# An ordered filter kept in memory, half of a transposition sent through memory, and scaled matrices made beside their use

## The chip, the cores and the metric

The kernel runs on one core of one Trainium2 chip. The metric is the device time of one execution in microseconds (us), as the median of several executions.

## The reference, cut to what matters

```python
def A(x, w_r, w_i):                       # spectral layer
    X = rfft2(x)                          # over S = 2048 and D = 1024
    X = X * (w_r + 1j * w_i)              # one filter, 2048 x 513
    return irfft2(X, s=(S, D)).astype(bf16)

def B(x, w1, b1, w2):                     # dense layer, F = 3584
    h = x @ w1 + b1
    return (h * tanh(log1p(exp(-abs(h))) + where(h > 0, h, 0))) @ w2

x = x + A(layernorm(x), w_r, w_i)
x = x + B(layernorm(x), w1, b1, w2)
x = x + A(layernorm(x), w_r, w_i)         # the same filter again
x = x + B(layernorm(x), w1, b1, w2)
```

All tensors are bf16. The second spectral layer uses the same filter as the first; this is what the first part of the change builds on.

## The kernel before

The transforms are matrix products with small tables. A spectral layer has a first step `s1`, then a software pipeline of 12 steps over 8 filter groups, then a last transform `i4` with the residual. In the first layer the layernorm's 1/std is folded into `s1` as 128 scaled copies of one 128x128 matrix. Helpers compute the waits of each operation from what it reads and writes. The helper for a DMA puts the DMA's waits into the program of the engine that issues it, so whatever comes later in that program stands behind them. In the trace GpSimd was held so for 10.2 us in two waits, 5.8 us the longest, by stores to xn_scratch.

```python
def first_scales(self):                   # first layer: statistics, then ALL scaled matrices
    ...
    for j in range(16):
        for q in range(8):                # every third on ScalarE, the others on VectorE
            ...  self.MN[n] = self.M0 * rc[n]

def load_w(g):                            # raw filter, ring of 4
    ...
    for c, src in enumerate((self.w_r, self.w_i)):
        rows = src.rearrange("(k s) d -> k s d", s=16)[:, a:b + 1:b - a, 1:513]
        self.dma(pool, wr.ap[:, c, :, :], rows, f"wr{g % 4}", parts=[wr.res])

def filter_bins(g):                       # raw filter -> ordered filter WT
    ...                                   # 12 matmuls of 128x64 turn a part around
    for i in range(2):
        ...
        self.op(pool, lambda e, d3=d3, lo=lo: e.tensor_copy(d3[:, :, :, 0:64], lo[:, :, 0:3, :]), ...)
        self.op(pool, lambda e, dd=dd, lo=lo: e.tensor_copy(dd, lo[:, :, 3:8:4, :]), ...)
        self.op(act, lambda e, d3=d3, src=src: e.activation(d3[:, :, :, 64:128], src, ACT.Copy), ...)

# s3: 4 matmuls (table FT), ScalarE evicts x, VectorE multiplies by the filter
    ta = x * wt[:, 0:1, :]; tb = x * wt[:, 1:2, :]      # two-input, 128x1024
    yk[:, 0] = ta[:, 0] - tb[:, 1]; yk[:, 1] = tb[:, 0] + ta[:, 1]
# i1 (table BT) and i2: inverse; VectorE evicts half 0 of U, ScalarE half 1

def u_turn(g, half):                      # row r of U becomes partition r*8+g of UT
    for i in range(8):
        r = 8 * half + i
        prog = sp
        if g == 7 and i % 2:
            prog = act
        elif g < 7 and i % 4 == 3:
            prog = pool
        self.dma(prog, self.UT.ap[r * 8 + g:r * 8 + g + 1, :, :], u.ap[:, r, :], ...)   # 32 KB

for step in range(8 + 4):
    g2, g3, g4, g5 = step, step - 1, step - 3, step - 4
    for h in range(2):
        s2(g2, h); filter_bins(g2) if h == 0; s3(g3, h); i1(g4, h); i2(g5, h); u_turn(g5, h)
    load_tabs(g3 + 2); load_w(g2 + 4); load_btabs(g4 + 2)     # all in GpSimd's queue
while self.w1_next < 28 * li + 4:
    self.load_w1()                        # first weights of the dense layer, SyncE
```

(Bounds checks are left out. Each u_turn row is a copy from SBUF to SBUF.)

## Time and profile before

| | before |
|---|---|
| median of 3, lowest, highest | 1152.24, 1148.83, 1152.91 us |
| span of the profiled execution | 1148.9 us |
| first step of layer 1 ends (first `s2` matmul) | 60.5 us |
| loop of layer 1, to its last inverse group / to `i4` | 91.6 / 17.8 us |
| from there to the first step of layer 2 (mainly dense 1) | 435.0 us |
| loop of layer 2 / to `i4` | 89.5 / 20.9 us |

The stage times are differences of start times in the timeline of TensorE. The list of waits has the engine, its line, what it waited for, then the sum, the count and the longest in us:

```profile
PE PS L700 <- DMA ARENA<-c_bt: 15.0, 4, 4.5
PE PS L813 <- DMA ARENA<-ARENA: 37.5, 2, 20.3
```

TensorE waits for tables (c_bt) in the loops, never for more than 4.5 us, and for up to 20.3 us at the end of a spectral layer, for the last rows of the turn.

### The profile page before, as it was taken

What the parts mean: (1) busy time and instruction counts of PE and PEld (TensorE: products, weight loads), DVE (VectorE), ACT (ScalarE), POOL (GpSimd) and SP (SyncE); (2) the same over time, 40 slices, a digit from 0 to 9 for tenths busy, and PEclk for the clock granted to TensorE, in tenths of its full rate; (3) what the DMA queues carried; (4) which work ended last, traced back from release to release, by engine and by line L of the source; (5) the groups of instructions that cost most, each with busy time, mean ns of one, the idle gap of its engine ahead of it and who ended that gap; (6) DMA issues with size and microseconds to landing.
All of it is one profiled execution on the core that took longest, in us unless ns stands there. A gap on an engine that the chain in (4) does not pass through costs nothing.

```text
span 1148.9 us, 14586 instructions
## 1 busy us (share of the span) xinstructions
PE 981.6 (85%) x6091; PEld 522.5 (45%) x6185; DVE 383.5 (33%) x813; ACT 332.9 (29%) x466; POOL 139.6 (12%) x204
## 2 busy tenths in 40 slices
PE   0388636999999999999958884489999999999998
PEld 0366524444444444444427663344444444444443
DVE  4877518250244400024326971546001110000111
ACT  6566515333100043400006662243320003442000
POOL 2165400000000000001343651000000000000000
PEclk9999968999999999999988997699999999999999
DMA  9634892344200022101971369713440002210000
GB/s 299 144 84 83 87 99 64 111 145 148 83 19 19 28 74 76 35 10 31 117 157 45 92 91 70 120 59 125 149 145 19 28 19 64 74 55 1 28 19 28
DMA packets 133105, 90.26 MB, mean 79 GB/s; under 512 B 56560, under 2 KB 114160, under 8 KB 133040
## 3 DMA queue, kind: packets, MB, share of 16 engines
q1 hardware_dynamic: 121600, 68.16, 25.3%
q0 software_dynamic: 8560, 20.52, 9.6%
q10 hardware_dynamic: 2880, 0.66, 1.3%
q8 instruction: 49, 0.80, 0.3%
q14 instruction: 16, 0.13, 0.0%
HBM read 72.46 MB, written 8.13 MB: 70 GB/s over the span
## 4 chain that ended last, share of the span: by engine, by line
PE 72%; DVE 13%; DMA 5%; SPq 4%; ACT 3%; issue 2%; ACTq 0%; POOL 0%; DVEq 0%
PE PS L886 33%; PE PS L868 32%; SPq L242 4%; DMA ARENA<-ARENA 2%; DMA XS<-in_A_x_dram 2%; DVE ARENA L682 2%; PE PS L605 1%; DVE ARENA L539 1%; PE PS L633 1%; DVE BN L427 1%; DVE XS L819 1%; PE PS L850 1%; DVE ARENA L689 1%; DVE ARENA L560 1%; DVE ARENA L684 1%
## 5 line engine op out<-in xcount | busy, mean ns | idle before, releaser
L868 PE MATMUL PS<-ARENA 128*128 128x512 bf16 x1752 | 385.3, 379 | 5.5 <-DVE ARENA L855 2.0
L886 PE MATMUL PS<-ARENA 128*128 128x512 bf16 x1754 | 387.4, 379 | 2.0
L872 ACT ACTIVATE ARENA<-PS,B 128x512 bf16<-128x512 f32 x224 | 153.6, 688 | 437.4 <-PE PS L868 437.4
L868 PEld LDWEIGHTS PS<-ARENA 128*128 128x128 bf16 x1792 | 174.4, 98 | 212.5 <-DVE ARENA L855 1.9
L886 PEld LDWEIGHTS PS<-ARENA 128*128 128x128 bf16 x1792 | 174.6, 98 | 207.7
L891 DVE TENSOR_TENSOR XS<-PS,XS 128x512 bf16<-128x512 f32 x64 | 44.3, 692 | 565.5 <-PE PS L886 565.5
L427 DVE BATCH_NORM_STATS2 BN<-XS 128x6 f32<-128x512 bf16 x104 | 67.1, 674 | 11.4 <-DMA XS<-in_A_x_dram 10.1
L242 POOL DMA_DIRECT2D ARENA<-xn_scratch x15 | 15.9, 1068 | 417.1 <-PE PS L886 388.3
L813 PE MATMUL PS<-MT,ARENA 128*128 128x32 bf16 (+1 forms) x768 | 24.6, 188 | 45.7 <-DMA ARENA<-ARENA 37.5
L819 DVE TENSOR_TENSOR XS<-PS,XS 128x512 bf16<-128x512 f32 (+1 forms) x40 | 29.1, 789 | 87.8 <-PE PS L813 87.8
L558 ACT ACTIVATE ARENA<-PS 128x1024 bf16<-128x1024 f32 x16 | 15.9, 1021 | 124.2 <-PE PS L552 124.0
L700 PE MATMUL PS<-ARENA 128*128 128x256 bf16 x256 | 37.5, 295 | 15.0 <-DMA ARENA<-c_bt 15.0
L813 PEld LDWEIGHTS PS<-MT,ARENA 128*128 128x128 bf16 x768 | 23.0, 101 | 49.1 <-issue 41.6
L408 ACT ACTIVATE ARENA<-XS 128x1024 bf16<-128x1024 bf16 x24 | 25.4, 1056 | 56.2 <-DVE XS L819 40.8
L707 ACT ACTIVATE ARENA<-PS 128x1024 bf16<-128x1024 f32 x32 | 32.6, 1020 | 24.1 <-PE PS L700 24.1
L700 PEld LDWEIGHTS PS<-ARENA 128*128 128x128 bf16 x256 | 26.6, 105 | 25.4 <-issue 15.8
L242 POOL DMA_DIRECT2D ARENA<-ARENA x56 | 30.2, 543 | 65.1 <-DVE ARENA L747 52.4
L682 DVE TENSOR_TENSOR ARENA<-ARENA 128x1024 bf16<-128x1024 bf16 x32 | 30.2, 943 | 23.1 <-ACT ARENA L678 23.0
L678 ACT ACTIVATE ARENA<-PS 128x1024 bf16<-128x1024 f32 x32 | 32.7, 1023 | 17.7 <-PE PS L674 17.7
L721 PE MATMUL PS<-ARENA,BD 128*128 128x256 bf16 x192 | 28.8, 293 | 9.5 <-DVE ARENA L747 9.2
L633 PE MATMUL PS<-FD,ARENA 128*128 128x256 bf16 (+1 forms) x312 | 34.0, 258 | 2.8 <-DVE ARENA L560 2.4
L613 POOL COPY ARENA<-ARENA 128x384 bf16<-128x384 bf16 x32 | 29.4, 920 | 10.4 <-DVE ARENA L684 10.4
(65 smaller groups left out, 621.6 us busy)
## 6 DMA issues: line engine op xcount, KB each, us to landing
ARENA<-in_B_w_dram SPq DMA_DIRECT2D x56, 512.0 KB, 3.9
ARENA<-in_B_w_dram SPq DMA_DIRECT2D x56, 256.0 KB, 4.5
ARENA<-ARENA SPq DMA_DIRECT2D x188, 32.0 KB, 6.6
XS<-in_A_x_dram SPq DMA_DIRECT2D x4, 1024.0 KB, 15.6
ARENA<-in_A_w_r_dram POOLq DMA_DIRECT2D x16, 256.0 KB, 4.1
ARENA<-in_A_w_i_dram POOLq DMA_DIRECT2D x16, 256.0 KB, 4.9
ARENA<-in_A_x_dram SPq DMA_DIRECT2D x32, 128.0 KB, 3.1
out_dram<-XS SPq DMA_DIRECT2D x16, 256.0 KB, 2.0
```

The costliest lines, as they stand in the source:

```text
L242: return eng.dma_start(out_ap, in_ap).then_inc(ds.sem, 16)
L427: self.op(self.dve, lambda e: e.bn_stats(self.BN[:, j, 6 * h:6 * h + 6], self.XS[:, j, 512 * h:512 * h + 512]), reads=[self.r_xs[j]], part ...
L633: fns.append(lambda e: e.matmul(dst, at(r), FD[:, t:t + dst.shape[-1] * 2], start=start, stop=stop))
L678: self.op(act, lambda e: e.activation(x.ap.rearrange("p a b -> p (a b)"), ps, ACT.Copy, scale=SIG), reads=banks, writes=[x.res])
L682: self.op(dve, lambda e: e.tensor_tensor(ta.ap, x.ap, wt.ap[:, 0:1, :].to_broadcast([P, 2, 512]), ALU.mult), reads=[x.res, wt.res], writes ...
L700: fns.append(lambda e, c=c, part=part: e.matmul(ps[:, c * 256:(c + 1) * 256], yk.ap[:, part, c * P:(c + 1) * P], t[:, (128, 0)[part]:(384, ...
L813: fns.append(lambda e, l=l: e.matmul(ps[:, w * l:w * l + w], self.UT.ap[:, u0 + l, :], self.MT[:, 8 * lo:8 * lo + w], start=True, stop=True))
L819: self.op(self.dve, lambda e: e.tensor_tensor(xs, src, xs, ALU.add), reads=rb, parts=self.r_xs[lo:lo + nb])
L868: fns.append(lambda e, db=db, bank=bank, fl=fl: e.matmul(PS[:, bank, :], wb.ap[:, db, fl * P:(fl + 1) * P], x.ap[:, db, :], start=(db == 0 ...
L872: self.op(act, lambda e, bank=bank, ft=ft: e.activation(at.ap[:, ft, :], PS[:, bank, :], ACT.Mish, bias=self.B1[:, ft:ft + 1]), reads=[sel ...
L886: fns.append(lambda e, i=i, ft=ft: e.matmul(PS[:, bank, :], at.ap[:, ft, t * P:(t + 1) * P], W2[ft].ap[:, h * 512:(h + 1) * 512], start=(i ...
L891: self.op(dve, lambda e: e.tensor_tensor(xs, PS[:, bank, :], xs, ALU.add), reads=[self.r_bank[bank]], writes=[self.r_xs[j]])
```

## The change

It has three parts. **Front:** the first filter loads wait until x is there, the statistics go ten to VectorE and six to ScalarE, and the scaled matrices are made four groups ahead inside `s1` instead of all before it; the ring of ordered filters grows from 4 to 8 buffers and that of raw ones shrinks from 4 to 2. **Kept filter:** during the first dense layer the filter is ordered once more, stored to memory, and loaded in order in layer 2, whose loop has no `filter_bins`. **Turn through memory:** for groups 0 to 6 the second half of the rows (eight of 16) is stored by SyncE to a scratch tensor, and one load by GpSimd brings it back onto eight partitions, in place of eight row copies. For odd groups ScalarE evicts half 0 as well.

```diff
 # front, s1
+        for j in range(4 if not li else 0):
+            self.scaled(j)
         for j in range(16):
             ...                                  # 8 matmuls, one eviction
+            if not li and j + 4 < 16:
+                self.scaled(j + 4)
 # rings
-        WT = ring("WT", 4, 2 * K, [2, 512])
+        WT = ring("WT", 8, 2 * K, [2, 512])
-        WR = ring("WR", 4, 4 * K, [2, 2, 512])
+        if li == 0:
+            WR = ring("WR", 2, 4 * K, [2, 2, 512])
 # layer 2 loads the ordered filter
+            self.dma(pool, ap.rearrange("p (a b c) -> p a b c", a=2, b=2), self.w_d[g], f"wt{g % 4}", reads=[self.r_wd[g]],
+                     writes=[w.res for w in pair])
-                if 0 <= g2 < 8 and h == 0:
+                if 0 <= g2 < 8 and h == 0 and li == 0:
                     filter_bins(g2)
 # turn
+            if half and g < 7:
+                self.dma(sp, self.u_d[g], u.ap[:, 8:16, :], f"uw{g % 3}", reads=[u.res], writes=[self.r_ud[g]])
+                self.dma(pool, self.UT.ap[64 + g:P:8, :, :], self.u_d[g].rearrange("l r n -> r l n"), f"um{g % 3}",
+                         reads=[self.r_ud[g]], parts=[self.UT.res])
+                return
 # dense layer 1
         for fg in range(14):
             mm1(2, fg)
             mm1(3, fg)
+            if not last and 2 <= fg < 10:
+                self.keep_filter(fg - 2)
+    def keep_filter(self, g):
+        ...
+        self.filter_bins(g, self.PS[:, 6:8, :]..., wr, ws, jt.ap, jt.res, self.dve)
+        self.dma(self.pool, self.w_d[g], ap, "ws", reads=[w.res for w in ws], writes=[self.r_wd[g]])
+        if g < 7:
+            self.load_wr(wr, g + 1)              # the one raw buffer is loaded again
```

(Moved buffers, new resources and the repeated body of `filter_bins` are left out.)

## The prediction

> **What bounds the kernel now.** I read the page's summary first: TensorE is busy 85% of the span. Then its chain of waits, to see where that is the whole story and where not.
>
> ```profile
> PE 72%; DVE 13%; DMA 5%; SPq 4%; ACT 3%; issue 2%; ACTq 0%; POOL 0%; DVEq 0%
> L868 PE MATMUL PS<-ARENA 128*128 128x512 bf16 x1752 | 385.3, 379 | 5.5 <-DVE ARENA L855 2.0
> L886 PE MATMUL PS<-ARENA 128*128 128x512 bf16 x1754 | 387.4, 379 | 2.0
> ```
>
> The two dense layers (some 200 to 589 us and 757 to 1149 us) are a solid run of matmuls: whatever is added to TensorE there is paid in full. The two spectral layers (0 to 170 us, 589 to 727 us) are the rest, and there the chain passes from engine to engine. In order of time it shows three places, of which the first is in the first layer only:
>
> ```profile
> 33.87 15.69 DVE ARENA L539 x96
> 49.56 1.14 DVE ARENA L560
> ...
> 595.04 9.35 DMA ARENA<-ARENA
> ...
> 683.91 4.84 DMA ARENA<-c_bt
> ...
> 702.52 1.97 SPq L242
> 717.69 8.87 DMA ARENA<-ARENA
> 727.71 4.63 DVE XS L819 x4
> ```
>
> First, all 128 scaled matrices are made before any eviction of the first step. Second, the last transposed rows of the input of layer 2 take 9.35 us to land, beside filter loads. Third, the inverse rows are turned by 128 row copies a layer, most issued by SyncE. SyncE's timeline:
>
> ```profile
> 648.88 69.41 SPq L242 DMA_DIRECT2D ARENA<-ARENA  x92
> ```
>
> Its issues are 0.645 us apart in the chain (0.60 and 0.04 of gap), so 12 rows a group take 7.7 us, and it is behind from 689 us to 718 us; the last row lands 8.9 us later and nothing runs meanwhile. Between these lies a loop of steps, one for each filter group; the chain of the window 117 to 175 us gives one turn:
>
> ```profile
> 116.94 1.05 PE PS L605 x9
> 118.01 0.87 ACT ARENA L619 x2
> 118.89 1.03 ACT ARENA L678
> 119.94 1.96 DVE ARENA L682
> 121.90 1.06 DVE ARENA L684
> 123.32 0.42 DVE ARENA L689
> 123.74 1.14 DVE ARENA L747
> 124.93 0.61 PE PS L721 x4
> ```
>
> A turn is 10.4 us. The filter ordering is in it twice openly (1.40 us for 12 matmuls of L605, 0.87 us of L619), and once hidden: L682 takes 1.96 us while GpSimd copies the filter, 0.68 us when it doesn't (timeline of VectorE).
>
> [...] The new load from memory has 8 destination partitions, [...] the existing loads of the transposed input have the same form and size, and two of them without a rush took 5.8 us to land against 3.7 us for a 192 KB table load[...].
>
> **Part by part.**
>
> *Loads and statistics, first layer.* Filter loads now wait for the last part of x, so x has the DMA engines alone. The windows show 384 to 408 GB/s between 10 and 20 us; 4.2 MB at 400 GB/s from 2 us is x complete by some 13.5 us, where the last group's statistics now begin after 25 us. Statistics: ten tiles on VectorE at 1.45 us, four folds of 0.6 us, from 5.2 us, with short waits: 22 us; the scales take 3.05 us (30.79 to 33.84). Scaling starts at 25 instead of 33.9 us: 8.9 us won. The rows of the transposed input (q1, about 200 GB/s at 30 to 50 us) should be in by 40 us, in quarters ahead of need.
>
> *Scaled matrices beside the step.* Nothing is removed: VectorE still has 15.7 us of scaling and 8 evictions of 1.15 us, 24.9 us in sum; the stage took 26.6 us (33.87 to 60.43). It had already overlapped some. 1.7 us won; VectorE is the bound. Both together: **-10 us**.
>
> *Keeping the filter.* Eight groups of 12 matmuls in the first dense layer, 1.40 us each by L605: **+11.2 us** on a solid TensorE. The rest hides if the single raw buffer comes back in time: matmuls 1.4, ScalarE 0.9, the store's issue 0.7, a load of two parts 0.7 + 3.8 to landing, 7.7 us after the start, against 8.3 us between groups (four times 1.73 us, plus 1.4). I count 0, at worst 1 us each.
>
> *Second layer, before the loop.* Eight filter loads of 1 KB runs become four of 4 KB, issued from 586 to 588 instead of up to 595.9 us; tables no longer wait for a buffer. The last input rows then share less: 6 us instead of 9.4: **-4 us**.
>
> *Second layer, loop, steps 0 to 4.* They take 33.7 us (616.2 to 649.9). Without L605, L619 and GpSimd's copies: step 0 is 2.2 us of matmuls; steps 1 to 3 go by VectorE, 4 multiplications of 0.6, 4 sums of 0.35, one eviction of 1.14, 5.2 us; step 4 by TensorE, 7.7 us; filling some 2 us. Sum 25.2 us: **-8.5 us**.
>
> *The turn, steps 5 to 11 and tail.* SyncE has 8 rows and one store a group, 9 times 0.645 is 5.8 us: no backlog. But GpSimd must wait for the store to land before it may issue the load back, and in its queue behind this come the table loads. Counted from a step's end T (last inverse matmul): rows from T-2.5 (the first half's eviction) to T+2.7, store issued T+3.3, landed T+6.8 (estimate: 2.0 us, the median of the same size, plus backlog), load issued by T+7.9, tables by T+9, landing behind that load at about T+15. They are needed two steps later, at the next T plus 2. With natural steps of 8 us that is T+10: a wait of 5 us in every second step, so some 10.5 us a step as before; then table waits of 2.5 and 8.5 us in the last steps (the old kernel has such waits too, 4.2 and 2.3 us). I arrive at step 10's end at +56 after step 4's, the last store at +64, its load landed at +70.5. The old kernel starts its last transform (L813) at 726.66, which is +76.8: **-6 us**.
>
> *The same in the first layer,* with the filter still in the loop (10 us a step; odd groups evict on ScalarE, about 1 us less): last load at +76 to +77, against 169.79 - 94.55 = 75.2: **+1 us**.
>
> Sum: -10 + 1 + 11.2 - 4 - 8.5 - 6 = -16.3 us; 1152.2 - 16.3 is 1136 us.
>
> **The rivals.** (a) The trip through memory becomes the bound[...]. Speaking for it: table loads that took 7 to 11 us in 124 to 142 us already stalled TensorE. Against: half the rows leave a queue whose landing times are 4.3 to 5.5 us while it isn't behind. If latencies are 3 us longer, both layers lose some 8 us: 1150 us. (b) The trip costs nothing, because store and load are quicker than I count: then steps run at 8 and 9.5 us and the tails shrink; 6 to 8 us won in each layer: 1121 us. (c) The kept filter stalls the dense layer by its single buffer: 8 us more, 1144 us. (d) The first layer gains nothing since the transposed input, not x, sets the start: it ended its issues at 42 us in the old kernel; then 5 us less gain: 1141 us.
>
> **Range and chances.** The gains that rest on counted work (-10, -8.5, +11.2) I trust to 3 us each; the turn is the open one, -13 to +14 us. Predicted 1136 us, 8 in 10 within 1117 to 1152. Faster by over 2% needs less than 1129.2 us, that is rival (b) in about half its size: 0.32. Slower by over 2% (over 1175) would need (a), (c) and (d) together: 0.03. Within 2%: 0.65.
>
> **What would show it.** In the changed profile: scaling starts near 25 us and the first step ends near 50 us (60.4 before); eight groups of 12 small matmuls in the first dense layer, 11 us, with no idle time of TensorE by a filter load; the second layer's steps 0 to 4 in about 25 us; the two-input multiplications of layer 2 near 0.68 us; TensorE waits in both layers named by the tables c_ft or c_bt, with GpSimd's queue waiting for the store to u_scratch, 4 us or more at a time. If there are no such waits and the loop of layer 2 runs at 8 us, I was wrong by rival (b); if the time between the last inverse matmul and L813 grows beyond 20 us, by (a).

## More of the kernel before

Most executions of a kernel here lie within 0.5% of its median. The ratio of an experiment is taken against executions of the kernel before that ran on the same chip in the same rounds. There were three such sets of rounds, e1 to e4 on one chip and e5 to e8 and e9 to e12 on another, with medians of 1152.07, 1150.1 and 1151.16 us for the kernel before; two experiments of different sets are compared through their ratios as well.

The groups of VectorE in the first layer's loop (60 to 102 us), with the count, the busy sum in us and the mean in ns of one (L682 and L684 are the multiplications by the filter, L687 and L689 the difference and the sum, L687 at 425 ns):

```profile
L689 DVE TENSOR_TENSOR ARENA<-ARENA 128x512 bf16<-128x512 bf16 x8 | 8.0, 998 | 0.0
L682 DVE TENSOR_TENSOR ARENA<-ARENA 128x1024 bf16<-128x1024 bf16 x9 | 8.0, 886 | 6.4 <-ACT ARENA L678 6.4
L684 DVE TENSOR_TENSOR ARENA<-ARENA 128x1024 bf16<-128x1024 bf16 x9 | 7.0, 778 | 0.0
```

## The result and the profile after

| | before | after |
|---|---|---|
| median of 4 | 1150.53 us | 1181.19 us |
| lowest to highest | 1147.51 to 1152.91 | 1176.97 to 1183.94 |
| span, granted clock of the profiled execution | 1148.9, 0.958 | 1182.1, 0.938 |

The changed kernel is correct and slower: 1.0265 times the time before (95% interval 1.0222 to 1.0307). A ratio here is the mean time of one kernel's runs over that of the other's of the same rounds, so it is not quite the ratio of the medians.

| stage, us | before | after | difference | predicted |
|---|---|---|---|---|
| to the first `s2` of layer 1 | 60.5 | 50.1 | -10.4 | -10 |
| layer 1, loop and tail | 109.3 | 132.7 | +23.4 | +1 |
| dense 1 and input of layer 2 | 435.0 | 448.8 | +13.8 | +11.2 - 4 |
| layer 2, loop and tail | 110.4 | 115.8 | +5.4 | -8.5 - 6 |

These sum to +32.2; the spans differ by 33.2 (1 us lies in the rest). The front came out as predicted; two of the other three lines are about 20 us worse. The page's summary of the chain:

```profile
PE 68%; DVE 13%; DMA 10%; ACT 2%; issue 2%; SPq 2%; POOL 2%; ACTq 0%; POOLq 0%; DVEq 0%
```

DMA has doubled its share (5% before), SyncE has halved its own (4% before) and GpSimd, absent before, has 2%. So the relief that was intended is there, and something else has taken more. The list of waits of the changed kernel tells what:

```profile
POOL ARENA L242 <- DMA u_scratch<-ARENA: 137.4, 14, 18.4
...
PE PS L692 <- DMA ARENA<-c_bt: 21.0, 4, 8.6
...
PE PS L663 <- DMA ARENA<-c_ft: 9.7, 2, 5.0
...
PE PS L818 <- DMA ARENA<-in_A_w_i_dram: 8.9, 5, 6.3
```

The first line is GpSimd, which waited 14 times, 9.8 us each on average, for a store to scratch to land before it could issue the load back. The others are TensorE, waiting for tables and raw filter parts, and these stand behind the load back in GpSimd's program. The chain of waits in the first layer's loop shows the two joined (start, duration, what):

```profile
93.77 2.39 DMA u_scratch<-ARENA
...
96.45 2.37 POOL ARENA L242 x3
98.81 7.51 DMA ARENA<-in_A_w_i_dram
...
106.37 1.55 PE PS L818 x12
...
121.91 2.36 DMA u_scratch<-ARENA
...
124.56 1.09 POOL ARENA L242
125.66 5.92 DMA ARENA<-c_ft
...
132.09 0.63 PE PS L664
...
143.58 2.51 DMA u_scratch<-ARENA
```

At 93.77 us the store has been issued; it lands; GpSimd issues the load back and the next loads of its queue; only then does the filter part or the table start, and TensorE runs 7.5 or 5.9 us later. What comes before, between 116.89 and 121.87 us in the same view, is SyncE issuing eight row copies, 0.60 us each with 0.04 us between, ahead of the store. The same chain leads from the table on to the next store, at 143.58 us, so that one lap takes 21.7 us; the lap after it, to the store at 164.17 us, takes 20.6 us. GpSimd's timeline says how long it stood still before the first of these loads, in brackets at the end of the line:

```profile
96.45 1.10 POOL L242 DMA_DIRECT2D ARENA<-u_scratch  x1 [18.36 <-DMA u_scratch<-ARENA]
```

From 78.1 to 96.45 us nothing behind this load could be issued. The tail of layer 2 in the chain:

```profile
738.41 6.48 DMA u_scratch<-ARENA
...
745.59 2.24 POOL ARENA L242 x3
...
748.36 9.94 DMA ARENA<-ARENA
```

Nothing in this kernel covers the last trip of a layer: from the store's issue at 738.41 us to `i4` at 758.75 us it is 20.3 us. The store takes 6.48 us to land and the load back 11.3 us (DMA view of 744 to 747 us), and the rows that GpSimd issues behind this load land last. From 742.88 us SyncE also issues the first weights of the dense layer. In the dense layer the kept filter shows up as predicted in kind:

```profile
437.88 1.56 PE PS L818 x12
439.52 0.88 ACT ARENA L832 x2
...
442.25 4.97 DMA ARENA<-in_A_w_i_dram
447.26 1.56 PE PS L818 x12
```

The round of one buffer (matmuls, ScalarE, issue, load) takes 9.4 us here, a little more than the 8.3 us between groups of large matmuls, so TensorE waits 0.5 to 0.9 us in four of the eight rounds.

### The profile page after: what moved, and what is told of

Its sections match the earlier page's. It is cut to its first block, busy times and chain, and to the rows that moved or that the text cites. A ratio compares the mean times of both kernels' runs of the same rounds, so it can differ in the third digit from the quotient of the medians.

```text
span 1182.1 us, 14518 instructions
## 1 busy us (share of the span) xinstructions
PE 1000.5 (85%) x6090; PEld 529.5 (45%) x6185; DVE 383.3 (32%) x843; ACT 335.4 (28%) x466; POOL 112.7 (10%) x155
## 3 DMA queue, kind: packets, MB, share of 16 engines
q0 software_dynamic: 11392, 31.19, 11.6%
## 4 chain that ended last, share of the span: by engine, by line
PE 68%; DVE 13%; DMA 10%; ACT 2%; issue 2%; SPq 2%; POOL 2%; ACTq 0%; POOLq 0%; DVEq 0%
PE PS L932 33%; PE PS L914 28%; DMA ARENA<-in_A_w_i_dram 3%; DMA u_scratch<-ARENA 2%; DMA ARENA<-ARENA 2%; DVE BN L431 2%; SPq L242 2%; DMA ARENA<-c_bt 1%; POOL ARENA L242 1%; DVE ARENA L572 1%; PE PS L896 1%; DVE ARENA L549 1%; PE PS L818 1%; DVE XS L865 1%; PE PS L692 1%
## 5 line engine op out<-in xcount | busy, mean ns | idle before, releaser
L431 DVE BATCH_NORM_STATS2 BN<-XS 128x6 f32<-128x512 bf16 x108 | 69.6, 674 | 7.4 <-DMA XS<-in_A_x_dram 6.2
L859 PEld LDWEIGHTS PS<-MT,ARENA 128*128 128x128 bf16 x768 | 22.8, 101 | 56.0 <-issue 48.9
L670 ACT ACTIVATE ARENA<-PS 128x1024 bf16<-128x1024 f32 x32 | 32.7, 1023 | 46.0 <-PE PS L666 46.0
L699 ACT ACTIVATE ARENA<-PS 128x1024 bf16<-128x1024 f32 x32 | 32.7, 1021 | 30.0 <-PE PS L692 30.0
L674 DVE TENSOR_TENSOR ARENA<-ARENA 128x1024 bf16<-128x1024 bf16 x32 | 24.5, 766 | 46.7 <-ACT ARENA L670 46.5
L412 ACT ACTIVATE ARENA<-XS 128x1024 bf16<-128x1024 bf16 x20 | 21.1, 1056 | 64.5 <-DVE XS L865 53.5
L625 PE MATMUL PS<-FD,ARENA 128*128 128x256 bf16 (+1 forms) x312 | 36.9, 273 | 2.6 <-DVE ARENA L572 2.4
L818 PE MATMUL PS<-ARENA 128*128 128x64 bf16 x192 | 24.8, 293 | 11.8 <-DMA ARENA<-in_A_w_i_dram 8.9
L713 PE MATMUL PS<-ARENA,BD 128*128 128x256 bf16 x192 | 30.9, 307 | 3.0 <-DVE ARENA L739 2.6
L625 PEld LDWEIGHTS PS<-FD,ARENA 128*128 128x128 bf16 x312 | 28.6, 106 | 9.7 <-DVE ARENA L572 2.9
L896 PE MATMUL PS<-IDENT,ARENA 128*128 128x128 bf16 x256 | 23.1, 252 | 9.5 <-DVE ARENA L474 7.8
```

Of the source, the lines that this page charges most:

```text
L431: self.op(self.dve, lambda e: e.bn_stats(self.BN[:, j, 6 * h:6 * h + 6], self.XS[:, j, 512 * h:512 * h + 512]), reads=[self.r_xs[j]], part ...
L625: fns.append(lambda e: e.matmul(dst, at(r), FD[:, t:t + dst.shape[-1] * 2], start=start, stop=stop))
L818: fns.append(lambda e, col=col, j=(j0 + c) * P, mov=mov: e.matmul(ps[:, col:col + 64], jt[:, j:j + P], mov, start=True, stop=True))
L859: fns.append(lambda e, l=l: e.matmul(ps[:, w * l:w * l + w], self.UT.ap[:, u0 + l, :], self.MT[:, 8 * lo:8 * lo + w], start=True, stop=True))
L896: fns.append(lambda e, db=db: e.transpose(PSb[:, bank, db * P:(db + 1) * P], xn.ap[:, db * P:(db + 1) * P], self.IDENT[:]))
```

## The experiments

**Theory.** The order in GpSimd's queue is the cause: the load back waits for a store that SyncE issues only after eight row copies, and the tables and raw filter parts behind it come too late. This is called Theory A in the expectations. **Rivals.** (1) The trip through memory is itself too slow or takes too much of the DMA engines; then its order would not matter. (2) The kept filter or the front is the cause: the dense layer's extra work, the smaller ring of raw filters. (3) Filter copies on GpSimd collide with VectorE now that the ring of 8 lets them run at other times. A stage time of one profile scatters: e1_rows and e5_front_alone below run the same code in layer 1's loop, which took 102.5 and 97.4 us. So stages are read to some 5 us.

The stages of all kernels, in us (the stage "dense 1" goes from `i4` to the first step of layer 2):

| kernel | first s2 | loop 1 | tail 1 | dense 1 | loop 2 | tail 2 |
|---|---|---|---|---|---|---|
| before | 60.5 | 91.6 | 17.8 | 435.0 | 89.5 | 20.9 |
| after | 50.1 | 111.2 | 21.6 | 448.8 | 91.9 | 23.9 |
| e1_rows | 50.0 | 102.5 | 19.2 | 452.1 | 77.0 | 21.8 |
| e2_memory_alone | 59.9 | 104.8 | 23.8 | 435.5 | 102.0 | 23.5 |
| e3_late_load | 50.2 | 82.6 | 27.6 | 448.8 | 66.9 | 26.4 |
| e4_no_keep | 50.1 | 113.1 | 23.4 | 434.9 | 110.0 | 21.8 |
| e5_front_alone | 50.1 | 97.4 | 17.6 | 434.8 | 92.3 | 22.8 |
| e6_store_first | 50.2 | 83.6 | 30.4 | 433.6 | 65.6 | 25.2 |
| e7_tail | 50.1 | 83.6 | 13.6 | 448.2 | 68.0 | 16.4 |
| e8_copies_vector | 50.2 | 74.3 | 27.8 | 449.2 | 62.2 | 28.1 |
| e9_all_three | 50.2 | 77.0 | 19.0 | 432.8 | 64.8 | 15.4 |
| e10_memory_late_alone | 60.7 | 75.8 | 25.1 | 435.4 | 76.0 | 30.9 |
| e11_before_queue | 60.8 | 83.8 | 29.7 | 435.6 | 83.1 | 30.2 |
| e12_all_but_memory | 50.1 | 81.4 | 18.0 | 431.5 | 68.4 | 18.3 |

### e1_rows: the changed kernel with the rows turned as before

```diff
-            if half == 0 and g % 2 == 0:
+            if half == 0:
...
-            if half and g < 7:
-                ...                                # store, load back
-                return
...
+                if g == 7 and i % 2:
+                    prog = act
+                elif g < 7 and i % 4 == 3:
+                    prog = pool
```

> The changed kernel with the inverse rows turned by row copies as before. Theory A (the trip through memory holds back the table and filter loads behind it in GpSimd's queue, and lengthens the tail): the first layer from the end of its first step to its last transform goes from 132.7 back to about 109 us, the second layer's same stretch from 115.8 to about 97 us (12 rows a group at 0.645 us on SyncE become its bound); total about 1140 us. Rival B (the kept filter and its loads are the main loss): at most 15 us less than the changed kernel, some 1167 us or more.

Measured: 1155.36 us against 1152.07 us, ratio 1.0028 (0.9998 to 1.0058). Without the memory turn the regression is gone, so the turn carries nearly all of it. The front and the kept filter together win nothing: in the stages, 10.5 us of the front and 11.6 us in layer 2's loop and tail against 17 us in dense 1 and 12 us in layer 1's loop and tail. The total was expected at about 1140 us and missed by 15 us: layer 2 came back as expected (98.8 us), layer 1 only to 121.7 us and not to 109 us. e5 and e8 look into that.

### e2_memory_alone: the kernel before with the memory turn and nothing else

The diff is that of the turn above, applied to the kernel before (with the eviction of odd groups on ScalarE and the three queues of group 7).

> The kernel before with the turn through memory alone (and its odd evictions on ScalarE). Theory A: slower than before by 25 to 40 us, 1176 to 1190 us, with GpSimd's waits for the store to u_scratch above 100 us and TensorE waiting for c_ft, c_bt. Rival B: within 10 us of before.

Measured: 1183.9 us, ratio 1.0275 (1.0251 to 1.0298). The turn alone makes the kernel as slow as the whole change. Its list of waits has GpSimd at the store for 126.3 us in 14 waits, and TensorE at c_bt for 20.8 and at c_ft for 18.7 us. Rival (2) can't be the main cause.

### e3_late_load: the load back issued one step later, behind that step's other loads

```diff
+        pending = []
+        def u_back(keep):
+            while len(pending) > keep:
+                g = pending.pop(0)
+                self.dma(pool, self.UT.ap[64 + g:P:8, :, :], self.u_d[g].rearrange("l r n -> r l n"), f"um{g % 3}",
+                         reads=[self.r_ud[g]], parts=[self.UT.res])
...
-                self.dma(pool, self.UT.ap[64 + g:P:8, :, :], ...)
+                pending.append(g)
...                                              # at the end of each step, after load_tabs, load_w, load_btabs
+            u_back(1 if step < 9 else 0)
```

The transfers are the same in number, size and form; only the place and time of 14 issues in one queue differ. (The run doesn't part 'behind the other loads' from 'one step later'.)

> The changed kernel, with all the trips through memory, but each load back is issued one step later and behind that step's table and filter loads in GpSimd's queue. Theory A in its form 'place in the queue': the waits in the loop go, 15 to 20 us less in each layer, total about 1145 us; the tail keeps its 23 us. Rival C (the trip itself is dear: its traffic on the DMA engines, whoever is queued behind): within 8 us of the changed kernel, 1173 us or more.

Measured: 1137.12 us, ratio 0.9879 (0.9852 to 0.9906), 44 us less than the changed kernel. TensorE's longest wait in the loop and tail of layer 1 (50 to 165 us) is now this one, and no table or filter is in the list at all:

```profile
PE PS L867 <- DMA ARENA<-ARENA: 27.0, 1, 27.0
```

GpSimd still waits for the stores, 77.0 us in all, but nothing urgent stands behind it. The loops lose 29 and 25 us against the changed kernel. This decides between the theory and rival (1) for the loops: there the trip is not too slow, it stood in the wrong place. The tails grew by 6 and 2.5 us, and the chain of the first one says why:

```profile
129.23 3.83 DMA u_scratch<-ARENA
...
142.01 4.17 DMA u_scratch<-ARENA
...
149.35 10.60 DMA ARENA<-ARENA
```

Here SyncE is behind. Its timeline has it issuing without a pause from 123.64 us, eight rows and a store a group in some 6 us, while the last inverse groups come 2 to 4 us apart. So the last store is issued at 142.01 us, 9 us after the last inverse group began, and the last rows, issued by GpSimd behind the load back, take 10.6 us to land. That last piece overlaps loads of dense weights, four of 512 KB with a median of 11.8 us to landing.

### e4_no_keep: the changed kernel with the filter ordered in both layers

```diff
-            if li == 0 and g2 + 2 < 8:
+            if g2 + 2 < 8:
                 load_w(g2 + 2)
...
-            if not last and 2 <= fg < 10:
-                self.keep_filter(fg - 2)
```

(and `filter_bins` in layer 2 again)

> The changed kernel with the filter ordered in the second layer too, none kept. Theory A: the first dense layer gets its 15 us back, but the second layer's loop carries the filter loads behind the trip as the first layer's does (132.7 against 115.8 us there), so about 17 us come back: total within 6 us of the changed kernel, 1175 to 1187 us. Rival B: 15 us or more below the changed kernel, under 1167 us.

Measured: 1189.13 us, ratio 1.0311 (1.0282 to 1.034), just outside the 1175 to 1187 us expected. Taking the kept filter out doesn't make the kernel faster; the median is 8 us higher, by the ratios 5 us, with intervals that overlap. Dense 1 gives back 13.9 us, and layer 2's loop takes 18 us more. So the kept filter was no cause of the loss; its gain is nearly paid off by its price in the dense layer.

### e5_front_alone: the kernel before with the front part alone

The diff is the front part of the change, with rings of 8 ordered and 2 raw filters in both layers.

> Only the first part of the change: deferred filter loads, two raw filter buffers, eight ordered ones, scaled matrices beside the first step; rows turned as before, the filter ordered in both layers. Theory D (GpSimd's filter copies now fall on VectorE's multiplications and slow them, because eight ordered buffers and the shifted loads no longer hold them back): the 10 us won by the end of the first step are given back in the loops, about 11 us in the first layer as in the run with rows, and some in the second; total 1150 to 1160 us. Rival E (the front is a clean gain and the loss in the run with rows comes from something else): about 1142 us.

Measured: 1154.03 us against 1150.1 us, ratio 1.0045 (0.9999 to 1.0092). The front's 10.4 us are there (first `s2` at 50.1 us) but don't come through: the loop of layer 1 is 5.8 us longer than before, that of layer 2 2.8 us, the last tail 1.9 us. In VectorE's groups of 50 to 92 us the multiplications by the filter, L678 and L680 here, take 867 and 1082 ns on average, against 886 and 778 ns in the kernel before; but the difference and the sum take 600 and 526 ns against 425 and 998 ns. Two of each are done for a group, 6.15 us in all against 6.17 us. So the slow instructions are others than before, and their sum is the same: these means alone don't show rival (3). e8 tests it.

### e6_store_first: e3, and the ordered filter stored in layer 1's loop instead of made again

```diff
+            if li == 0 and g2 < 8:
+                pair = WT[2 * g2 % 8:2 * g2 % 8 + 2]
+                ...
+                self.dma(pool, self.w_d[g2], ap..., "ws", reads=[w.res for w in pair], writes=[self.r_wd[g2]])
...
-            if not last and 2 <= fg < 10:
-                self.keep_filter(fg - 2)
```

> The late-load version, but the ordered filter is stored from the first layer's own ordering, by one store per group from GpSimd's queue, and nothing is ordered in the first dense layer. Theory F (the kept filter costs its matmuls and waits in the dense layer, 13.8 us by the stages, and nothing else): first dense stretch 435 instead of 449 us, first loop within 4 us of 82.6, total about 1123 us. Rival G (the stores get in the way of the table loads in the first loop): loop over 90 us, total 1131 us or more.

Measured: 1121.61 us, ratio 0.9759 (0.9726 to 0.9791), 15.5 us less than e3 (14 us by the ratios). Dense 1 falls from 448.8 to 433.6 us, and layer 1's loop pays no more than the scatter (83.6 against 82.6 us, its tail 2.8 us more). The ordering in the dense layer was work that the kernel had already done once; eight stores of 512 KB cost nearly nothing where they stand now.

### e7_tail: e3, and the ends of the turn treated by themselves

```diff
-            if half and g < 7:
+            if half and g < 6:
...
+                if g >= 6:
+                    prog = (sp, pool)[i % 2] if half == 0 else (sp, act, pool, sp)[i % 4] if g == 6 else (act, act, pool, sp)[i % 4]
+                elif i % 4 == 3:
+                    prog = pool
...
-            self.load_w1()
+            self.load_w1(after=[self.UT.res])      # dense weights wait for the rows
```

> The late-load version; groups 6 and 7 turned by rows alone, shared among SyncE, GpSimd and ScalarE; the other row copies shared with GpSimd as before; the first dense weights are loaded only when all rows have landed. Theory H (the tail is the last group's trip behind SyncE's rows and the weight loads): each tail from 27 to about 19 us, total about 1121 us. Rival I (the row copies themselves saturate the DMA engines at the end): tails stay above 24 us, total 1132 us or more.

Measured: 1120.23 us, ratio 0.9756 (0.9719 to 0.9793), 16.9 us less than e3 (14 us by the ratios). The tails fall from 27.6 and 26.4 to 13.6 and 16.4 us, the loops by nothing. The last two groups by rows on three queues, and the weights behind them, end the layer sooner than a trip does. The run doesn't part the two (fewer trips at the end, later weights).

### e8_copies_vector: e3, and the copies of the filter in layer 1 by VectorE

```diff
-            self.filter_bins(g, ..., self.JT, self.r_jt, pool)
+            self.filter_bins(g, ..., self.JT, self.r_jt, dve)
```

> The late-load version with the first layer's filter copies on VectorE instead of GpSimd. Theory D: VectorE has 1.6 us more work a group, but its multiplications run at 0.68 us instead of up to 1.94, so the time from the first step's end to the first inverse group's end falls from about 40 to 35 us or less, total about 1132 us. Rival J (VectorE is simply full there, contention is a side matter): the first loop grows by up to 10 us, total 1140 to 1147 us.

Measured: 1130.13 us, ratio 0.9835 (0.9797 to 0.9874), 7 us less than e3 (5 us by the ratios, with intervals that overlap, so the total alone doesn't settle it). VectorE has more instructions and is done sooner. Its groups of the window 50 to 92 us, first in e3, from which this kernel differs by this edit alone:

```profile
L676 DVE TENSOR_TENSOR ARENA<-ARENA 128x1024 bf16<-128x1024 bf16 x7 | 10.5, 1503 | 0.0
L674 DVE TENSOR_TENSOR ARENA<-ARENA 128x1024 bf16<-128x1024 bf16 x7 | 7.3, 1046 | 5.8 <-ACT ARENA L670 5.8
```

and in this kernel:

```profile
L674 DVE TENSOR_TENSOR ARENA<-ARENA 128x1024 bf16<-128x1024 bf16 x10 | 6.9, 687 | 3.7 <-ACT ARENA L670 3.7
L676 DVE TENSOR_TENSOR ARENA<-ARENA 128x1024 bf16<-128x1024 bf16 x9 | 6.2, 685 | 0.0
...
L834 DVE COPY ARENA<-ARENA 128x384 bf16<-128x384 bf16 x12 | 6.0, 499 | 0.0
```

Four copies of a group take 1.77 us on VectorE (two of 499 and two of 386 ns), and 3.51 us on GpSimd in e3 (1008 and 747 ns). In return the multiplications are 359 and 818 ns shorter, and the difference and the sum 201 and 122 ns (626 and 540 ns in e3, 425 and 418 ns here). Two of each are done for a group, so this gives back 3.0 us, more than the price, and the filter is ready sooner besides; the run doesn't part the two.

What it does to the loop is clearest in its opening, from the first `s2` to the end of the first inverse group. In layer 1 the 14 profiles fall into three sets that don't overlap:

| kernels | copies by | opening, us |
|---|---|---|
| before, e2, e10, e11 | GpSimd, rings as before | 34.1 to 35.9 |
| after, e1, e3, e4, e5, e6, e7 | GpSimd, changed rings | 37.8 to 42.4 |
| e8, e9, e12 | VectorE, changed rings | 32.7 to 33.6 |

So rival (3) is right as a part: the opening was 2 to 8 us longer with the new rings, and it is short again once the copies are off GpSimd (41.9 us in e3, 33.6 us in e8). In layer 2, where no scaled matrices are made, e4 and e5 have it too (39.0 and 37.2 us against 33.6 us before). Whether the ring of 8, the ring of 2 or the moved buffers bring it about, no run separates. (Layer 2's loop, with the same code in e3 and e8, differs by 4.7 us; that counts as scatter here.)

### e9_all_three: e3 with the edits of e6, e7 and e8

The diff is the sum of the three above.

> The late-load version with all three repairs: filter stored from the first layer's ordering, last two groups by rows on three queues with the weights held back, filter copies on VectorE. If the parts add: 1137 - 15.5 - 17 - 7 = 1098 us, loops 75 and 66, tails 14 and 16, first dense stretch 434 us. If they share one cause, 1105 us or more.

Measured: 1094.8 us against 1151.16 us, ratio 0.9509 (0.947 to 0.9547). It beats both kernels: by 4.9% the one before, by some 7% the changed one (1181.19 us). The three edits give 15.5, 16.9 and 7.0 us over e3 one by one, 39.4 us in sum, and 42.3 us together (by the ratios 33 us in sum, 43 us together). So none of them takes away what another wins. In TensorE's waits of its loop and tail in layer 1 (48 to 150 us) only the end of the turn is left above 3 us:

```profile
PE PS L875 <- DMA ARENA<-u_scratch: 18.3, 1, 18.3
PE PS L692 <- DMA ARENA<-c_bt: 2.7, 3, 1.7
```

### e10_memory_late_alone: the kernel before with the memory turn in its late order

The diff is that of e2 with the `pending` list of e3.

> The kernel before with the trip through memory alone, loads back issued late. Theory A (place in the queue): against the same trip issued early (1183.9 us) each loop is 23 us shorter, about 80 us; the tails are some 27 us, 7 longer than before; total about 1142 us. If the filter part was needed for the gain of the late load: 1160 us or more.

Measured: 1139.15 us, ratio 0.9893 (0.9854 to 0.9932), where e2 was at 1183.9 us with the same transfers. The order of 14 issues is worth 45 us here too. With e3 (1137.12 us) this also weighs the rest of the change: in the late order front and kept filter together add 2 us of gain, which is within the scatter: the front's 10.5 us and 13.6 us of layer 2's loop and tail against 13.4 us in dense 1 and 9.3 us in layer 1's loop and tail.

### e11_before_queue: the kernel before, with GpSimd's own row copies issued behind its loads

```diff
+                if prog is pool:
+                    rows_later.append((g, r))
+                    continue
...                                              # end of the step, after its loads
+            u_rest()
```

> The kernel before, with no part of the change: only GpSimd's row copies (4 of 16 of a group) are issued behind the step's loads of tables and filters. If the old kernel has the same fault of order in a small form, its waits for c_bt (15 us in all) shrink and each loop falls by 3 to 6 us: 1140 to 1146 us. If the old loop is bound by its chain alone: within 3 us of before.

Measured: 1156.41 us, ratio 1.0033 (0.9993 to 1.0072), a miss: I had thought that the loads' place in the queue might be the whole gain of e10. The loops do get shorter, by 7.8 and 6.4 us, and the waits for c_bt fall from 15.0 to 2.3 us, but the tails grow by 11.9 and 9.3 us. In the chain from 690 to 735 us, up to layer 2's `i4`, SyncE's issues alone are 70.6%. With 12 rows a group SyncE is still behind; a loop that runs sooner only reaches this bound sooner. So the order explains why the change lost, but it doesn't give what e10 wins: as long as SyncE keeps 12 rows a group, the trip through memory is worth 17 us (e11 against e10). e12 shares the rows otherwise.

### e12_all_but_memory: e9 without the trip through memory

```diff
-            if half and g < 6:
-                ...                                # store, load back later
-                return
...
+                elif i % 2:
+                    prog = pool
+                if prog is pool:
+                    rows_later.append((g, r))
+                    continue
```

(Rows are shared by SyncE and GpSimd, eight each, GpSimd's behind its loads.)

> As the run with all three repairs, but no trip through memory: 16 rows a group, half on SyncE and half on GpSimd behind its loads, the last two groups on three queues. If the trip itself is worth something (it takes 8 rows a group off the issue, at 0.645 and 0.54 us each, and off the DMA engines): 8 to 15 us slower than that run, by longer tails. If it is worth nothing once the order is right: within 4 us of it.

Measured: 1102.26 us, ratio 0.9554 (0.9509 to 0.9599), between the two expected cases. The trip, which cost 31 us as it was built, is worth some 6 to 7 us in the best version (1094.8 us), not far above the scatter, and most of the 56 us that the best version gains on the kernel before doesn't need it.

## Why the prediction was wrong, by its own steps

**The front: right.** VectorE starts the scaled matrices at 25.34 us (25 predicted) and `s1` ends at 50.1 us (50), 10.4 us won. Between them lie 24.8 us, the work of VectorE that the prediction took for the bound (24.9 us). The timeline of VectorE in the changed kernel:

```profile
25.34 4.00 DVE L549 TENSOR_SCALAR ARENA<-ARENA 128x128 bf16<-128x128 bf16 x24
29.25 1.22 DVE L572 CAST ARENA<-PS 128x1024 bf16<-128x1024 f32 x1
```

**Layer 1's loop, "odd groups evict on ScalarE, about 1 us less", "+1 us": wrong by 22 us, in two terms.** The opening, from the first `s2` to the end of the first inverse group, took 40.3 us (50.1 to 90.5) against 34.1 us before (60.5 to 94.6): +6.2 us, for which the prediction had nothing. It had read from the kernel before that L682 takes 1.96 us beside GpSimd's copies, and had not asked what other rings do to those copies. That the copies on GpSimd are the cause is shown by e8's table of openings; how they lengthen it only with the new rings stays open. From there to `i4` it took 92.4 us, with 76 to 77 predicted and 75.2 before: +17 us, the turn.

**"The turn, steps 5 to 11 and tail": the step that failed.** Its mechanism was named, GpSimd waiting for the store and tables behind it, and the waits predicted in kind are in the trace. The start of a trip was right too: predicted at T+3.3, the stores were issued at T+1.8 to T+5.1 in layer 2 and at T+2.8 to T+5.4 in layer 1. What failed is the size of the sum. For layer 2 the prediction has step 10's end at +56 after step 4's, the last store at +64, its load landed at +70.5. Measured: +64.7, +76.3 (landed) and +88.3, and the last rows behind that load landed at +89.7. These are two terms of about 9 us.

First, the steps, +8.7 us. TensorE's waits for tables in this layer's loop were 20.2 us (4.6, 5.0, 1.9 and 8.6), about what was predicted (5 us in every second step, then 2.5 and 8.5). But the prediction let steps 9 and 10 be short: at its 10.5 us a step the four steps before them come to 42 us (44.9 measured), which leaves 14 us, and they took 19.8 us. The laps in the chain say why: a late table delays the next inverse group, whose rows and store then come later, and with them the next load and table; such a lap took 20.5 us at the end too (717.89 to 738.41 us). The prediction also had no term for slower matmuls after a wait. The same 128x512 matmul takes 0.38 us in the quiet part of layer 2's loop and 0.63 us after the wait of 4.64 us that ends at 681.65 us, while the granted clock is 0.50 (682 to 688 us; 1.00 until 679 us and again from 691 us). On the chain the matmuls of 681.65 to 689.96 us and of 727.76 to 731.34 us take 10.8 us, where the same groups take 5.3 us at full clock: 5 to 6 us of the 8.7 us, an estimate from these lines. No run changes the clock alone. Here the clock fell some 3 us after TensorE stopped at 677.0 us and came back some 9 us after it had started again (both estimates, worked out from mean clocks of 0.69 in 679 to 682 us and 0.60 in 688 to 691 us).

Second, the last trip: from step 10's end to its load landed 23.6 us, where 14.5 us were predicted. The store took 6.48 us to land (3.5 predicted) and the load back 11.3 us, in layer 1 11.4 us, where the other 12 loads took 5.6 to 6.7 us. In both layers SyncE was issuing the weights of the dense layer at that time. e7, which holds these weights back and makes no trip for the last groups, has tails of 13.6 and 16.4 us.

In layer 1 a third term comes in. The time was worked out for the tables alone, but the raw filter, with its ring cut from 4 to 2, stands in the same queue and had no reserve: the load for a later group was issued after GpSimd's wait of 18.36 us and cost TensorE 6.3 us.

**What the prediction could have asked.** GpSimd stood still for 137.4 us in 14 waits, 4.9 to 18.4 us each, until a store had landed, and issued nothing meanwhile. The prediction had these waits ("4 us or more at a time"), but treated a queue with a wait in it as a delay of a few microseconds instead of asking which of its entries could be moved ahead of the wait at no price. e3 did exactly this, for -44 us.

**Layer 2's loop, steps 0 to 4: right.** They took 25.6 us (643.0 to 668.6), with 25.2 predicted and 33.7 before. The closeness is partly luck: the terms as written (2.2, three times 5.2, 7.7 and 2) add to 27.5 us, not to 25.2. L674 and L676 are at 688 and 684 ns in this layer, as predicted (0.68 us).

**Layer 2's turn: wrong by 20 us.** From there to `i4` it took 90.2 us, with 70.5 predicted and 76.8 before. TensorE waited 10.5 us for c_bt and 9.7 us for c_ft in this layer; the last trip then took 23.9 us from the last inverse group to `i4`, over the 20 us that the prediction had given as the sign of rival (a). This sign was a weak one: the kernel before already had 20.9 us there.

**The kept filter: right in kind, short by 4 us in size.** The first half of the dense layer's last stretch, from the first of the later matmuls to the second product, took 111.8 us against 96.7 us: +15.1 where +11.2 was predicted. The 12 matmuls cost 1.40 to 1.56 us, not 1.40, which is about 12.2 us for eight, and 2.6 us are waits for the single buffer.

**"Second layer, before the loop", -4 us: about a third of it came.** The last input rows took 8.04 us to land (6 predicted, 9.35 before).

**The range and the chances.** Rival (a) was described rightly and given 8 us in each layer (1152 us in sum, not the 1150 written); against the prediction's own figures it took 16 and 20 us. The range up to 1152 us, and 0.03 for slower, took three rivals together to be needed; rival (a) alone took 36 of the 45 us by which the result missed 1136 us, because the laps set the pace of the loop to its end.

**What stays open.** The load back of 256 KB takes 5.6 to 6.7 us to land in 12 of 14 cases; the store of the same size lands after 2.4 to 2.6 us in six of 14 cases and after up to 6.5 us in the others. Whether the load back is slow because it fills only 8 partitions, or by its 256-byte pieces, or because tables and rows are beside it, no run separates.

## What to carry to other kernels

A DMA that must wait for another one belongs behind everything in its queue that is ready and needed soon: 14 issues moved one step back turned +2.7% into -1.2%. Before you recompute a thing in order to keep it, look for the place where it already exists and store it there (some 15 us). When a copy is moved to a second engine to relieve the first, compare the mean of the first one's instructions with and without it: here VectorE was faster when it did the work itself (3.0 us of a group given back for 1.8 us of copies).
